# Attention's landmark chain moved to earlier half steps in a fused attention and expert kernel

## The chip, the cores and the metric

The kernel runs on one core of one Trainium2 chip. The metric is the device time of one execution, in microseconds (us); less is better. The core has five engines that run side by side, each through its own queue in order: TensorE (matmuls, PE in the profile; its weight loads are PEld), VectorE (DVE), ScalarE (ACT), GpSimd (POOL) and SyncE (SP), which issues DMAs here.

## The reference

Nyström attention (B = 8, H = 8, S = 576, D = 64, 32 landmarks), then two feed-forward layers:

```
q_lm = q.reshape(B, H, m, S // m, D).mean(axis=3)
k_lm = k.reshape(B, H, m, S // m, D).mean(axis=3)
A = sm(q, k_lm)
Bm = sm(q_lm, k_lm)
C = sm(q_lm, k)
Z = Bm.transpose(0, 1, 3, 2) / (np.linalg.norm(Bm, ord=1, ...) * np.linalg.norm(Bm, ord=np.inf, ...) + 1e-06)
for _ in range(6):
    Z = 2 * Z - Z @ Bm @ Z
x = A @ Z @ C @ v
...
h = (x @ w1) * (x @ w2) @ w3 @ w_out
...
g = elu(h @ w_in2)
out = g @ w_out2
```

All data are float32; sm is the scaled softmax over the last axis.

## The kernel before

The program has three stages. The **start** (to about 120 us) loads and converts the first weights, forms w3 times w_out, and runs the attention of batch 0 in between. The **fused stage** (to about 675 us) goes through 8 batches of 16 units each: a unit multiplies one piece of attention by its own weights (`ab`, lines 695 to 697, 12 matmuls of 288 columns), multiplies the two results (`ab_product`: copy `a` on ScalarE, line 704, product `g` on VectorE, line 706), splits the product of the unit before in two parts (`ab_split`: `gh` on ScalarE, `gl` on VectorE, lines 70 and 71), and multiplies the parts of two units before by w3 (`yy`, lines 722 to 724, 12 matmuls). The **last stage** is the second layer, in 512-token blocks.

While the units of batch b run, the attention of batch b+1 is worked out in pieces, called half steps, two to a unit: the even one stands between `ab` and `yy`, the odd one after `yy`. The table in `steps` says which piece stands at which half step; there is no scheduler behind it, each engine's queue follows from the order in which the program is written. The pieces that matter here:

- `sums` and `q_pad`: landmark sums of queries and keys (VectorE, line 302), their padded copy (ScalarE, line 308).
- The landmark chain: `b_scores` (TensorE, line 353, then maximum and difference on VectorE, lines 359 and 361), `b_exp` (ScalarE, line 365), `b_soft` (four operations on VectorE, lines 371 to 374), `b_norms` (five, lines 378 to 385), `b_norms2` (five, lines 391 to 399), `r0` (TensorE, line 406; X on VectorE, line 408), six times `newton` (`n` on TensorE, line 418; X on VectorE, line 420).
- The keys' part: `c_scores` in two halves (TensorE, line 317; copies `e` on ScalarE, line 328), `c_max` in two (VectorE, lines 334 and 335), `c_exp` in two (ScalarE, line 338), `c_trans` in three (`ct`: TensorE, lines 429 and 432; copy on ScalarE), `c_norm` (VectorE, lines 345 and 347), then `cv` and `zcv`, which join both parts.
- From step 22 on, the queries' scores `a_scores` (line 317 for `a`, transposes at line 488).

`r0` and those Newton steps that fall on an even half step are taken ahead of the rest by `quick`, between `ab` and `ab_product`. Beside the attention, `fill` moves a pipe of weight conversions on by one tick in each half step. A conversion (`join_bits`) starts at half steps 1, 5, 11, 14 and 18 and has its four VectorE operations (lines 169 to 172) three ticks later, at 8 for the one that starts at 5; its GpSimd operations follow one tick after. In the start, the steps of batch 0 run at 1.6 per tick beside `bits_job` (lines 120 to 133). The scores, r0, Newton steps and transposes share two PSUM buffers (pool `ps_at`), taken in turn; `ab` has two others, which the copy `a` and the product `g` free.

Of the kernel before, what the change touches and what calls it, by code (L numbers as in the profile page):

```python
# [64 lines left out]
def nystrom_moe_kernel(ctx, tc, qT, kT, vm, vr, w12, w3T, w_out1, w_in2, w_out2, out):  # L65
# [216 lines left out]
    class Attention:  # L282
# [239 lines left out]
        def steps(self, first=False):  # L522

            s = {}

            def at(i, f, *a):
                s.setdefault(i, []).append((f, a))

            for hp in range(NP):
                at((-16, -14, -12, -11)[hp], self.sums, "k", hp)  # L530
                at(hp, self.sums, "q", hp)
            at(4, self.q_pad)
            at(6, self.b_scores)
            at(7, self.b_exp)
            at(7, self.c_scores, 0)
            at(8, self.c_scores, 1)
            at(8, self.b_soft)
            at(9, self.c_max, 0)
            at(9, self.c_exp, 0)
            at(10, self.b_norms)  # L540
            at(10, self.c_max, 1)
            at(10, self.c_exp, 1)
            at(11, self.b_norms2)
            at(12, self.r0)
            at(13, self.c_norm)
            for k in range(6):
                at(13 + k, self.newton, k)
            for k in range(3):
                at(11 + 2 * k, self.c_trans, k)
            at(18, self.cv, 0)  # L550
            at(19, self.cv, 1)
            at(21, self.zcv)
            when = ((22, 22, 23, 24, 25, 26, 27), (26, 27, 28, 29, 30, 32, 34))
            if first:
                when = ((11, 11, 12, 13, 14, 15, 16), (17, 17, N1, N1 + 1, N1 + 2, N1 + 3, N1 + 4))
            for n, o in enumerate(when):
                at(o[0], self.a_scores, n)
                at(o[1], self.a_max)
                at(o[2], self.a_sub)
                at(o[3], self.a_exp)  # L560
                at(o[4], self.a_sum)
                at(o[5], self.a_mul, n)
                at(o[6], self.a_split, n)
            return s
# [6 lines left out]
    with tc.manual_schedule():  # L571
# [55 lines left out]
        for o in ORDER:  # L627
            if o == "A":
                k, n_wo = n_wo, n_wo + 1
# [389 lines left out]
```

## Time and profile before

| | us |
|---|---|
| median of 3 runs | 1438.42 |
| lowest, highest | 1437.57, 1439.11 |
| the profiled execution | 1436.56 |
| its span, first to last instruction | 1434.4 |

| engine | busy, us | share of the span |
|---|---|---|
| TensorE (PE) | 1370.2 | 96% |
| weight loads (PEld) | 1179.0 | 82% |
| VectorE (DVE) | 1088.0 | 76% |
| ScalarE (ACT) | 630.8 | 44% |
| GpSimd (POOL) | 368.3 | 26% |

Matmuls overlap in the profile, and their ends are modelled: a busy TensorE there is not TensorE at its peak, and the gaps between matmuls say more than the share. A row of a timeline has the start, the length, the engine, the line, the operation, what it writes and reads, and in brackets the idle time of the engine ahead of it with what ended it.

### The profile page before, as it was taken

To read this page: it belongs to the slowest core of one execution; us is meant where nothing else is said; L and a number is where in the kernel's file an instruction comes from. 1 tells how busy PE (TensorE), PEld (TensorE's weight loads), DVE (VectorE), ACT (ScalarE), POOL (GpSimd) and SP (SyncE) were. 2 spreads that over 40 slices of the span, in tenths; PEclk is the share of its full clock that TensorE was granted. 3 is DMA by queue.
4 is the path that set the end of the run, shared out by engine and by line. 5 is a ranking of instruction groups with operands and counts; after the bars stand their busy time and mean duration, and the time that the engine had idled before them with its cause. 6 is when DMAs were issued, how large, how long until landed. Compare 5 with 4: busy or idle time off the path is not lost.

```text
span 1434.4 us, 27127 instructions
## 1 busy us (share of the span) xinstructions
PE 1370.2 (96%) x10848; PEld 1179.0 (82%) x10848; DVE 1088.0 (76%) x2003; ACT 630.8 (44%) x1266; POOL 368.3 (26%) x378
## 2 busy tenths in 40 slices
PE   5786999999999999999999999999999999999998
PEld 2234888888878888899898989999899998999987
DVE  7898687778687787744887878878687887877774
ACT  5444454435344444433444434444344444434442
POOL 4452346344365353420301101010110101011000
PEclk9988999999999999999999999999999999999999
DMA  8643344453635533252966465565645556555440
GB/s 308 234 137 122 121 156 168 165 165 108 207 101 189 204 127 112 102 200 74 414 250 225 165 226 193 188 229 185 210 179 211 207 185 219 198 196 195 177 161 30
DMA packets 56014, 259.70 MB, mean 181 GB/s; under 512 B 5200, under 2 KB 14416, under 8 KB 43600
## 3 DMA queue, kind: packets, MB, share of 16 engines
q0 software_dynamic: 12672, 140.51, 27.2%
q1 hardware_dynamic: 43216, 117.46, 23.5%
q8 instruction: 85, 1.39, 0.4%
q14 instruction: 41, 0.34, 0.1%
HBM read 216.01 MB, written 41.94 MB: 180 GB/s over the span
## 4 chain that ended last, share of the span: by engine, by line
PE 83%; DVE 13%; ACT 1%; issue 1%; DMA 1%; SPq 0%; DVEq 0%; ACTq 0%
PE o L857 9%; PE o L856 9%; PE o L855 9%; PE hm L800 8%; PE hm L801 8%; PE hm L802 8%; PE y L722 5%; PE ab L695 4%; PE ab L696 4%; PE ab L697 4%; PE y L724 4%; PE y L723 4%; PE m L317 2%; DVE w_b L128 1%; DVE w_b L124 1%
## 5 line engine op out<-in xcount | busy, mean ns | idle before, releaser
L800 PE MATMUL hm<-yb,wh 128*128 128x256 f32 x1008 | 285.3, 283 | 3.6 <-ACT s L812 3.5
L801 PE MATMUL hm<-yb,wh 128*128 128x256 f32 x1008 | 285.1, 283 | 0.0
L802 PE MATMUL hm<-yb,wh 128*128 128x256 f32 x1008 | 284.9, 283 | 0.0
L857 PE MATMUL o<-wo,el 128*128 128x512 f32 x576 | 225.6, 392 | 0.0
L856 PE MATMUL o<-wo,eh 128*128 128x512 f32 x576 | 225.3, 391 | 0.0
L855 PE MATMUL o<-wo,eh 128*128 128x512 f32 x576 | 224.0, 389 | 0.0
L831 ACT ACTIVATE t<-m 128x512 f32<-128x512 f32 x144 | 89.9, 624 | 301.4 <-DVE m L829 301.4
L800 PEld LDWEIGHTS hm<-yb,wh 128*128 128x128 f32 x1008 | 192.9, 191 | 6.9 <-ACT s L812 4.0
L746 POOL DMA_DIRECT2D wh<-wh_d x72 | 39.5, 549 | 613.6 <-PE hm L802 607.5
L801 PEld LDWEIGHTS hm<-yb,wh 128*128 128x128 f32 x1008 | 192.9, 191 | 2.8
L802 PEld LDWEIGHTS hm<-yb,wh 128*128 128x128 f32 x1008 | 193.0, 192 | 0.0
L722 PE MATMUL y<-gh,w3oh 128*128 128x288 f32 x512 | 160.5, 313 | 2.9 <-DVE w3ol L71 2.9
L834 DVE SCALAR_TENSOR_TENSOR t<-m,t 128x512 f32<-128x512 f32 x144 | 99.2, 689 | 77.9 <-ACT m L832 77.9
L695 PE MATMUL ab<-ath,mh 128*128 128x288 f32 x512 | 157.2, 307 | 0.9 <-ACT a L704 0.9
L696 PE MATMUL ab<-atl,mh 128*128 128x288 f32 x512 | 151.8, 296 | 0.0
L697 PE MATMUL ab<-ath,ml 128*128 128x288 f32 x512 | 151.1, 295 | 0.0
L724 PE MATMUL y<-gh,w3ol 128*128 128x288 f32 x512 | 151.0, 295 | 0.0
L723 PE MATMUL y<-gl,w3oh 128*128 128x288 f32 x512 | 150.8, 295 | 0.0
L722 PEld LDWEIGHTS y<-gh,w3oh 128*128 128x128 f32 x512 | 96.1, 188 | 39.9 <-issue 22.3
L857 PEld LDWEIGHTS o<-wo,el 128*128 128x128 f32 x576 | 108.1, 188 | 22.7
L855 PEld LDWEIGHTS o<-wo,eh 128*128 128x128 f32 x576 | 108.5, 188 | 20.9
L856 PEld LDWEIGHTS o<-wo,eh 128*128 128x128 f32 x576 | 108.1, 188 | 21.2
(146 smaller groups left out, 2732.4 us busy)
## 6 DMA issues: line engine op xcount, KB each, us to landing
wh<-wh_d POOLq DMA_DIRECT2D x72, 1792.0 KB, 7.8
wo_raw<-in_w_out_dram SPq DMA_DIRECT2D x24, 512.0 KB, 5.4
k<-in_kT_dram SPq DMA_DIRECT2D x8, 1152.0 KB, 6.4
q<-in_qT_dram SPq DMA_DIRECT2D x8, 1152.0 KB, 5.3
yd<-ysb SPq DMA_DIRECT2D x16, 576.0 KB, 3.6
yin<-yd SPq DMA_DIRECT2D x9, 1024.0 KB, 9.9
out_dram<-osb SPq DMA_DIRECT2D x36, 256.0 KB, 2.3
w_raw<-in_w3T_dram SPq DMA_DIRECT2D x16, 512.0 KB, 5.1
```

Source lines behind the costliest of these rows:

```text
L695: pe.matmul(p[:, :NH], mh[:, cs], ah[:, blk, :], start=(blk == 0), stop=False)
L696: pe.matmul(p[:, :NH], mh[:, cs], al[:, blk, :], start=False, stop=False)
L697: pe.matmul(p[:, :NH], ml[:, cs], ah[:, blk, :], start=False, stop=(blk == 1))
L722: pe.matmul(a[oc][:, :NH], w3o_hi[fc][:, os_], gh, start=(fc == 0), stop=False)
L723: pe.matmul(a[oc][:, :NH], w3o_hi[fc][:, os_], gl, start=False, stop=False)
L724: pe.matmul(a[oc][:, :NH], w3o_lo[fc][:, os_], gh, start=False, stop=(fc == K1 - 1))
L800: pe.matmul(o, ah, bh[:, kk, :], start=(kk == 0), stop=False)
L801: pe.matmul(o, ah, bl[:, kk, :], start=False, stop=False)
L802: pe.matmul(o, al, bh[:, kk, :], start=False, stop=(kk == 1))
L855: pe.matmul(a, eh[:, ts_], w[:, 0, :], start=first, stop=False)
L856: pe.matmul(a, eh[:, ts_], w[:, 1, :], start=False, stop=False)
L857: pe.matmul(a, el[:, ts_], w[:, 0, :], start=False, stop=last)
```

## The change

Only numbers in the table of half steps change. The landmark chain moves forward: `b_scores` from 6 to 5, `b_exp` from 7 to 6, `b_soft` from 8 to 7, `b_norms` from 10 to 8, `b_norms2` from 11 to 9, `r0` from 12 to 10, the Newton steps from 13 to 18 to 11 to 16. The transposes `c_trans` move back from 11, 13, 15 to 12, 14, 16 and `c_norm` from 13 to 17. `c_scores`, `c_max` and `c_exp` keep their numbers, but at step 9 `b_norms2` is now written ahead of `c_max`.

```
-            at(6, self.b_scores)
-            at(7, self.b_exp)
+            at(5, self.b_scores)
+            at(6, self.b_exp)
+            at(7, self.b_soft)
             at(7, self.c_scores, 0)
+            at(8, self.b_norms)
             at(8, self.c_scores, 1)
-            at(8, self.b_soft)
+            at(9, self.b_norms2)
             at(9, self.c_max, 0)
             at(9, self.c_exp, 0)
-            at(10, self.b_norms)
+            at(10, self.r0)
             at(10, self.c_max, 1)
             at(10, self.c_exp, 1)
-            at(11, self.b_norms2)
-            at(12, self.r0)
-            at(13, self.c_norm)
             for k in range(6):
-                at(13 + k, self.newton, k)
+                at(11 + k, self.newton, k)
             for k in range(3):
-                at(11 + 2 * k, self.c_trans, k)
+                at(12 + 2 * k, self.c_trans, k)
+            at(17, self.c_norm)
```

VectorE in a steady batch (the attention of batch 3), from the end of the weight conversion at half step 8 (`w_s`, line 172) on; `cb` is the keys' maximum, `bt`, `bst`, `bsb`, `bsx` the first part of the norms. Before:

```order
L172 TENSOR_SCALAR w_s<-w_p 128x512
L334 TENSOR_REDUCE cb_3285<-e_3_3210 128x1
L335 TENSOR_SCALAR cb_3285<-cb_3285 128x1
L706 TENSOR_TENSOR g_3308<-ab_1_3299,a_3306 128x288
L71 TENSOR_TENSOR gl_3245<-g_3242,gh_3244 128x288
L378 STREAM_TRANSPOSE bt_3314<-bm_3195 128x64
L380 TENSOR_REDUCE bst_3316<-bm_3195 128x2
L381 TENSOR_REDUCE bst_3316<-bt_3314 128x2
L383 COPY bsb_3319<-bst_3316 128x128
L385 STREAM_TRANSPOSE bsx_3321<-bsb_3319 128x128
L334 TENSOR_REDUCE cb_3285<-e_3_3211 128x1
```

The same place in the change; `bmm` and `brc` are the second part of the norms, and the second X is the one from r0:

```order
L172 TENSOR_SCALAR w_s<-w_p 128x512
L391 TENSOR_REDUCE bmm_3294<-bsx_3260 128x4
L394 TENSOR_TENSOR brc_3296<-bmm_3294 128x2
L395 TENSOR_SCALAR brc_3296<-brc_3296 128x2
L396 RECIPROCAL brc_3296<-brc_3296 128x2
L399 TENSOR_TENSOR X_3300<-bm_3168,brc_3296 128x2x32
L334 TENSOR_REDUCE cb_3302<-e_3_3215 128x1
L335 TENSOR_SCALAR cb_3302<-cb_3302 128x1
L408 TENSOR_TENSOR X_3300<-r_3_3323,brc_3296 128x2x32
L706 TENSOR_TENSOR g_3335<-ab_1_3316,a_3333 128x288
L71 TENSOR_TENSOR gl_3250<-g_3247,gh_3249 128x288
L334 TENSOR_REDUCE cb_3302<-e_3_3216 128x1
```

The first part of the norms now stands ahead of the conversion, and the second part, the first maximum and X stand between the conversion and the next unit's product.

ScalarE at the same place in the change, from the copies of the keys' second scores on; `w_t` belongs to the conversion, and line 338 is the exponential that waits for `cb`:

```order
L328 COPY e_3_3215<-c_3_3262 128x288
L328 COPY e_3_3216<-c_3_3263 128x288
L167 ACTIVATE w_t<-w_raw 128x512
L338 ACTIVATE e_3_3215,csum_3303<-e_3_3215,cb_3302 128x576
L704 COPY a_3333<-ab_0_3309 128x288
L70 CAST gh_3249<-g_3247 128x288
L338 ACTIVATE e_3_3216,csum_3303<-e_3_3216,cb_3302 128x576
L704 COPY a_3398<-ab_0_3373 128x288
```

This order is as before up to the second exponential; a copy of `ct` that stood behind it is now further back.

TensorE in the start, where the second half of the queries' scores `a` begins. Before:

```order
L585 MATMUL w3acc_442<-wo_311,w_672 128x512
L585 MATMUL w3acc_443<-wo_311,w_672 128x512
L418 MATMUL n_0_733<-X_693 32x64 x8
L317 MATMUL a_0_745<-q_155,ksum_247 32x288
L317 MATMUL a_0_746<-q_155,ksum_247 32x288
```

And in the change:

```order
L432 MATMUL ct_0_718<-ident,e_0_381 64x128
L585 MATMUL w3acc_449<-wo_311,w_687 128x512
L585 MATMUL w3acc_450<-wo_311,w_687 128x512
L585 MATMUL w3acc_451<-wo_311,w_687 128x512
L585 MATMUL w3acc_452<-wo_311,w_687 128x512
L317 MATMUL a_0_756<-q_155,ksum_247 32x288
```

A Newton step stood right ahead of the scores; now all six are over by then.

## Rows read from the trace of the kernel before

**Rows 1.** TensorE's waits, 170 to 600 us: total, times, longest (us).
```profile
PE n L418 <- DVE X L408: 4.5, 4, 1.7
...
PE ct L429 <- ACT e L338: 2.8, 3, 1.3
```

**Rows 2.** Timeline of TensorE in the batch at 256 to 325 us.
```profile
285.07 0.60 PE L429 MATMUL ct<-ident,e 128*128 128x128 f32 x4
...
287.17 0.33 PE L406 MATMUL r<-bt 32*32 32x32 f32 x16
...
290.93 0.43 PE L418 MATMUL n<-X 32*32 32x64 f32 x16 [1.65 <-DVE X L408]
```

**Rows 3.** Timeline of VectorE in the same batch.
```profile
280.47 0.21 DVE L371 TENSOR_REDUCE bsum<-bm 128x2 f32<-128x64 f32 x1
...
281.26 0.29 DVE L169 TENSOR_SCALAR w_y<-w_y 128x512 uint16<-128x512 uint16 x1
...
282.71 0.29 DVE L172 TENSOR_SCALAR w_s<-w_p 128x512 uint16<-128x512 uint16 x1
282.92 0.74 DVE L334 TENSOR_REDUCE cb<-e 128x1 f32<-128x576 f32 x1
...
285.87 0.24 DVE L378 STREAM_TRANSPOSE bt<-bm 128x64 f32<-128x64 f32 x1
...
286.91 0.71 DVE L334 TENSOR_REDUCE cb<-e 128x1 f32<-128x576 f32 x1
```

**Rows 4.** Timeline of VectorE in the start, behind a conversion.
```profile
72.55 0.28 DVE L391 TENSOR_REDUCE bmm<-bsx 128x4 f32<-128x128 f32 x1
72.86 0.93 DVE L394 TENSOR_TENSOR brc<-bmm 128x2 f32<-128x2 f32 x1
73.83 1.20 DVE L395 TENSOR_SCALAR brc<-brc 128x2 f32<-128x2 f32 x1
...
75.40 0.84 DVE L488 STREAM_TRANSPOSE at<-a 128x288 f32<-128x288 f32 x2
```

**Rows 5.** Timeline of GpSimd at the same time.
```profile
72.17 1.60 POOL L133 TENSOR_TENSOR w_sb<-w_b,w_r 128x512 uint32<-128x512 uint32 x1 [5.19 <-DVE w_b L128]
```

**Rows 6.** Timeline of VectorE in the batch at 468 to 537 us.
```profile
501.84 0.28 DVE L391 TENSOR_REDUCE bmm<-bsx 128x4 f32<-128x128 f32 x1
...
502.89 0.22 DVE L408 TENSOR_TENSOR X<-r,brc 128x64 f32<-128x64 f32 x1
```

**Rows 7.** Timelines of ScalarE (a copy) and TensorE (a waiting ab).
```profile
284.72 0.38 ACT L704 COPY a<-ab 128x288 f32<-128x288 f32 x1
...
403.26 0.40 PE L695 MATMUL ab<-ath,mh 128*128 128x288 f32 x1 [0.93 <-ACT a L704]
```

**Rows 8.** Timelines of VectorE and TensorE, first and last of six batches.
```profile
215.60 0.29 DVE L172 TENSOR_SCALAR w_s<-w_p 128x512 uint16<-128x512 uint16 x1
...
217.76 0.66 PE L429 MATMUL ct<-ident,e 128*128 128x128 f32 x4
...
564.88 0.29 DVE L172 TENSOR_SCALAR w_s<-w_p 128x512 uint16<-128x512 uint16 x1
...
567.27 0.60 PE L429 MATMUL ct<-ident,e 128*128 128x128 f32 x4
```

**Rows 9.** TensorE's waits in the start, 40 to 118 us.
```profile
PE a L317 <- ACT ct L434: 4.2, 1, 4.2
PE a L317 <- DVE X L420: 3.6, 1, 3.6
```

**Rows 10.** Timeline of VectorE in the start, transposes of the second scores.
```profile
99.91 0.85 DVE L488 STREAM_TRANSPOSE at<-a 128x288 f32<-128x288 f32 x2 [1.34 <-PE a L317]
```

**Rows 11.** Windows: stretch, busy time (count) of PE, PEld, DVE, ACT, POOL; clock, DMA.
```profile
94.00:106.00 12.00, 7.74 (x95) 3.67 (x95) 10.62 (x21) 4.29 (x7) 5.27 (x5) 0.72 0.42 144
130.00:136.00 6.00, 4.98 (x31) 3.51 (x31) 5.86 (x11) 4.08 (x9) 2.60 (x2) 0.72 0.61 176
170.00:600.00 430.00, 417.79 (x4593) 357.76 (x4594) 333.22 (x734) 195.13 (x465) 205.15 (x199) 1.00 0.45 155
```

## The prediction

> **What bounds the kernel now.** I read the list of busy shares first, then TensorE's waits in the stretch of the steady batches, then one batch in the timelines of TensorE, VectorE, ScalarE and GpSimd, and last the start. TensorE sets the time of the fused stage: its matmuls there follow each other at a fixed pitch, and only where another engine is late does a gap open. So the worth of the change in batches 2 to 7 is the sum of such gaps before and after. The waits of TensorE between 170 and 600 us [rows 1] hold two that belong to the landmark chain: the first Newton step n waits for X, line 408, 4.5 us in four batches, and the first key transpose ct waits for the exponential e, line 338, 2.8 us in three. Together 7.3 us, which is all that the change can take away there. The third large wait, m for "at" (line 488), belongs to steps 22 and later, which stay.
>
> [Rows 2] show one batch: ct at half step 11, r0 between, then n, 1.65 us late for X. VectorE is late there because within two half steps it has to pass norms, a maximum, the second part of the norms, and then X.
>
> **What moves, and what VectorE then has in its queue.** The steps keep their instructions; no DMA is added or taken away, and the queues of SP and POOL hold the same rows. What changes is the place relative to a step that does not move: the weight conversion, whose four VectorE operations stand at the end of half step 8 (lines 169 to 172). Before, the softmax stood ahead of the conversion, and the maximum of the keys' first half (line 334) right behind it. Now the first part of the norms stands ahead, and behind the conversion come the second part of the norms, then the maximum, then X from r0. That is so in all six batches 2 to 7. So X, which n at half step 11 wants, and the maximum, for which the exponential waits, are both behind more work than before. I work out when the next unit's ab can start, from the start of L172, the conversion's last operation:
>
> - Softmax out, norms in ahead of the conversion: 281.26 - 280.47 = 0.79 us out, 286.91 - 285.87 = 1.04 us in: 0.25 us later [rows 3].
> - From L172 to the operation behind it: 282.92 - 282.71 = 0.21 us [rows 3].
> - Second part of the norms: the trace has it right behind a conversion once, in the start: from 72.55 to 75.40, 2.85 us [rows 4]. It is long because GpSimd takes up its own addition of the same conversion at 72.17, and the small operation at line 394 (0.93 us for 128x2) ends as that one ends, 72.17 + 1.60 = 73.77 [rows 4, 5]; the next one, line 395, takes 1.20 us. In a quiet place the same piece, from line 391 to X, is 502.89 - 501.84 = 1.05 us [rows 6]. Lower end 1.05, upper 2.85 and another wait; in the new order the piece follows the conversion directly, as in the start, so I take 2.85.
> - From the maximum to the end of the exponential, where ScalarE goes on to the copy a of the unit: 284.72 - 282.92 = 1.80 us [rows 3, 7]. That copy stands behind the exponential in ScalarE's queue in both kernels, and the next ab needs the PSUM bank that a reads.
> - The copy itself 0.38 us; at 403.26 the trace has an ab that waited for just such a copy [rows 7].
>
> Sum 0.25 + 0.21 + 2.85 + 1.80 + 0.38 = 5.49 us after the old start of L172. n itself can go earlier, when X is done, so the copy a is the later of the two and sets the gap.
>
> TensorE would be ready for that ab at the old start of ct (less the wait it had) plus r0 and n, which now stand ahead, 0.33 + 0.43 = 0.76 us [rows 2]. So the batch of [rows 2, 3] comes out at 282.71 + 5.49 - 285.07 - 0.76 = 2.37 us late; the first of the six at 215.60 + 4.73 - 217.76 = 2.57, the last at 564.88 + 4.73 - 567.27 = 2.34 [rows 8]. Worked out so, the six sum to 17.7 us (2.3 to 3.9 each). Against the 7.3 us that go: +10.4 us.
>
> Nothing hides this: the matmuls behind a waiting n stood too, as the gap of 1.65 us shows [rows 2]. What is late next is the second Newton step. Behind the late copy VectorE has the product g, its remainder gl, the second maximum, and only then n's update; this ends about as ab ends. If GpSimd holds gl as it held line 394 (up to 0.93 us), the second step waits that much; four of the batches have more GpSimd work queued then, and I take half of it for each, +2 us, between 0 and 4. From half step 12 on the Newton steps keep their spacing against the conversions as before, and the transposes have three and four half steps after their exponentials where they had two and three: nothing there. The reciprocal of the sums, moved from 13 to 17, lies beside a queue that has room, and its user comes at 19: nothing. The scores at 5 need the queries' padded sums of step 4, and the running maximum of 32 columns fits into VectorE's pause ahead of the next g: nothing.
>
> One rule of the Trainium skill bears on the 2.85 us. It says (page "SBUF — State Buffer", section "SBUF: two separate sides") that VectorE and GpSimd share a port pair as an exclusive lock, held for a whole instruction, taken by whichever starts first, and asked for by a VectorE operation with two SBUF inputs or in a two-port mode. Line 394 ending with GpSimd's addition agrees. By that rule line 399, with two inputs, would be caught a third time wherever GpSimd has a third operation queued, as in four of the six batches; at 0.93 us each that is +3.7 us on the sum, which I leave to the range.
>
> **The start.** Steps run 1.6 to a conversion there. The one wait that goes cleanly is at half step 17: the scores a of the second half hold on for the update of a Newton step, 3.6 us [rows 9], because that step holds a PSUM buffer and its update stands behind a conversion. Now Newton is over by 16. But VectorE reaches the transposes of a only after the same conversion: they waited 1.34 us for TensorE [rows 10], less 0.21 us for a small operation that now stands ahead (a step of this size is in [rows 3]): -1.1 us, counted as if all of it reaches the end of the start. The wait of a for ct, 4.2 us [rows 9], goes too, but the longer norms behind the earlier conversion and a transpose queue of equal length take its place; I set it at nothing, and bound the start by -7.8 (both waits) and +2 us. Batch 1, whose conversions are others, I set at nothing, within 1 us either way.
>
> **Sum.** 10.4 + 2 - 1.1 = 11.3 us. On the profiled execution, 1436.56 us, that is 1447.9; the median of the runs shown, 1438.42, stands 1.86 us above it, so 1449.7 us.
>
> **Rivals.**
> *The port is free.* If GpSimd's additions start later than VectorE's small operations, the second part of the norms takes 1.05 us. Each batch is then 1.80 us less late, 17.7 - 10.8 = 6.9, 0.4 less than what goes away; with the start 1438.42 - 0.4 - 1.1 = 1436.9 us. Against it: the two orders in which the engines arrive are 0.1 us apart and VectorE came second in the start. It decides at line 394.
> *The start pays.* If the start ends as soon as TensorE has its scores, both waits there, 4.2 + 3.6 = 7.8 us, come off. With the price of the forecast this is still 10.4 + 2 - 7.8 = +4.6, 1443.0 us; with a free port too it is 1438.42 - 0.4 - 7.8 = 1430.2 us, faster. It needs VectorE to have room in the start, and it is nearly always busy there, so this is unlikely.
> *The clock falls.* After the 3.6 us wait of a [rows 9], the stretch from 94 to 106 us shows a granted clock of 0.72 on average, between the levels of 2.4 and 1.2 GHz, which is 12 x 0.28 = 3.4 us lost; 130 to 136 shows 0.72, 1.7 us lost [rows 11]. The new gaps of 2.3 to 3.9 us are of that size, with only n's small matmuls in them. Three falls at 1.7 to 3.4 would give 1454.8 to 1459.9, six short ones 1459.9. Against it: from 170 to 600 us, with the waits of [rows 1] in it, the clock stands at 1.00 [rows 11]. The Trainium skill speaks for it (page "TensorE: Matmul & The Clock Gate", section "HAM oscillation — how this bites in real kernels"): bursts parted by waits bring the engine back slow each time; no steady batch here shows it yet.
>
> **How the numbers follow.** Forecast 0.58, clock 0.22, free port 0.12, the start with a free port 0.08. About 0.2% (2.9 us) is what a measurement of this kernel can tell from no change. Slower by more: forecast and clock and a little of the free port, 0.82; within: 0.10; faster: 0.08. The range goes from 1440, a port that is free in most batches, to 1461, six falls of the clock.
>
> **What would show it.** TensorE's wait of n for X should be there in all six batches, 2 us or so, followed by a wait of ab for a of 0.5 to 1; the wait of ct for e gone; lines 394, 395 at 0.5 to 1.2 us each right behind line 172; start of the fused stage about 1 us earlier. Wrong if n's wait vanishes, if lines 394 and 395 take below 0.2 us, or if the start moves by more than 3 us.

## The result and the profile after

The changed kernel takes 1454.39 us (median of 4 runs, 1452.42 to 1455.96); the kernel before, in the same comparison, 1437.99 us (1437.44 to 1439.11). The ratio is 1.0116, with a 95% interval of 1.0101 to 1.0132: slower by 16 us, where 1449.7 us was forecast, in a range of 1440 to 1461. The profiled execution took 1455.96 us with a span of 1454.2 us, 19.8 us more than the span before; it is the slowest of the four.

TensorE's waits in the changed kernel, 170 to 615 us, are the first thing to set beside [rows 1] (who waits for whom, then total, times and longest, in us):

```profile
PE n L418 <- DVE X L408: 11.3, 6, 2.6
PE ab L695 <- ACT a L704: 4.2, 7, 0.9
```

The wait of ct for e is gone, as the change meant it. The wait of n for X went from 4.5 us in four batches to 11.3 in all six, and a second one came behind it: ab for the copy a, 0.9 us before (the one row with it in [rows 7]), 4.2 now. So TensorE stands 7.6 us longer in those six batches: 6.8 for n, 3.3 for ab, 0.3 for the second Newton step (n for X at line 420), less the 2.8 of ct.

VectorE in the batch of [rows 2, 3], now some 4 us later, from the conversion's last operation on (start, length, operation):

```profile
286.88 0.29 DVE L172 TENSOR_SCALAR w_s<-w_p 128x512 uint16<-128x512 uint16 x1
287.09 0.28 DVE L391 TENSOR_REDUCE bmm<-bsx 128x4 f32<-128x128 f32 x1
287.40 1.09 DVE L394 TENSOR_TENSOR brc<-bmm 128x2 f32<-128x2 f32 x1
288.53 0.17 DVE L395 TENSOR_SCALAR brc<-brc 128x2 f32<-128x2 f32 x1
288.74 0.17 DVE L396 RECIPROCAL brc<-brc 128x2 f32<-128x2 f32 x1
288.94 0.87 DVE L399 TENSOR_TENSOR X<-bm,brc 128x64 f32<-128x64 f32 x1
289.73 0.74 DVE L334 TENSOR_REDUCE cb<-e 128x1 f32<-128x576 f32 x1
...
290.58 0.21 DVE L408 TENSOR_TENSOR X<-r,brc 128x64 f32<-128x64 f32 x1
```

GpSimd at the same time:

```profile
287.32 1.16 POOL L174 TENSOR_TENSOR w_t<-w_t,w_s 128x512 f32<-128x512 f32 x1 [5.79 <-DVE w_s L172]
288.56 1.16 POOL L176 TENSOR_TENSOR wx<-w_t,w_p 128x512 f32<-128x512 f32 x1
```

The operation at line 394, two numbers per partition, starts 0.08 us after GpSimd's first operation and ends as that one ends (287.32 + 1.16 = 288.48). Line 395 then starts at 288.53, 0.03 us ahead of GpSimd's second operation, and takes its own 0.17 us; line 399 falls into that second one and ends 0.09 us behind it. So the second part of the norms, from 287.09 to 289.73, takes 2.64 us, and X comes after the maximum. The other five batches show the same lengths to 0.02 us.

ScalarE and TensorE there:

```profile
290.75 0.78 ACT L338 ACTIVATE e<-e,cb 128x576 f32<-128x576 f32 x1 [5.14 <-DVE cb L335]
...
291.53 0.38 ACT L704 COPY a<-ab 128x288 f32<-128x288 f32 x1
```

```profile
290.94 0.43 PE L418 MATMUL n<-X 32*32 32x64 f32 x16 [1.28 <-DVE X L408]
291.96 0.40 PE L695 MATMUL ab<-ath,mh 128*128 128x288 f32 x1 [0.59 <-ACT a L704]
```

n is 1.28 us late for X, and the ab behind it another 0.59, because ScalarE waited 5.14 us for the maximum, with the copy a behind it in its queue.

The waits are 7.6 of the 19.8 us. The rest shows in the windows (stretch, busy times with counts, then clock, DMA share, GB/s): five falls of the granted clock between 170 and 620 us, each in its stretch of 10 us, against none between 170 and 600 us before [rows 11].

```profile
220.00:230.00 10.00, 9.40 (x100) 8.43 (x98) 4.08 (x13) 4.64 (x13) 0.00 (x0) 0.83 0.19 75
360.00:370.00 10.00, 8.01 (x77) 7.09 (x78) 4.32 (x13) 4.11 (x10) 4.37 (x5) 0.66 0.78 249
440.00:450.00 10.00, 9.47 (x99) 8.65 (x100) 4.61 (x12) 4.25 (x13) 1.38 (x3) 0.83 1.01 354
510.00:520.00 10.00, 6.81 (x76) 5.84 (x78) 5.58 (x15) 4.12 (x10) 1.71 (x2) 0.83 0.36 142
580.00:590.00 10.00, 8.16 (x89) 7.12 (x88) 7.39 (x18) 3.39 (x9) 7.20 (x8) 0.84 0.20 54
```

Each lies right behind one of the late n. Apart from the waits of n and ab, TensorE is busy there, but at 1.2 GHz for a part: 10 x (0.17 + 0.34 + 0.17 + 0.17 + 0.16) = 10.1 us lost. Only the batch at 290 us kept its clock. A sixth fall came in the last stage, where a wait that the kernel before has too (2.77 us, hm for s) took the clock down in this execution and not in that one:

```profile
692.00:710.00 18.00, 14.95 (x93) 14.40 (x94) 14.86 (x26) 8.09 (x15) 6.39 (x12) 0.81 0.98 355
```

At the first matmul of that stage that waits (hm for s, 0.76 us in both) the changed kernel is 692.28 - 674.78 = 17.5 us behind; the stage itself takes 2.3 us more (1454.2 - 692.28 against 1434.4 - 674.78). 7.6 + 10.1 + 2.3 = 20.0, against 19.8 us. The 2.3 are not laid to the change: the clock falls at that wait in ten of the thirteen profiles here, with either table, and not in three, the kernel before among them. The start and batch 1 together come out at 0.25 us less (the first y, line 722, of the 17th unit, just ahead of batch 2's chain, starts at 204.36 before and 204.11 now), and that hides two parts. TensorE at the start of the fused stage, before and after:

```profile
127.96 0.40 PE L722 MATMUL y<-gh,w3oh 128*128 128x288 f32 x1 [0.65 <-DVE w3ol L71]
...
150.72 0.66 PE L429 MATMUL ct<-ident,e 128*128 128x128 f32 x4 [2.18 <-DVE ml L479]
```

```profile
125.17 0.40 PE L722 MATMUL y<-gh,w3oh 128*128 128x288 f32 x1 [0.65 <-DVE w3ol L71]
...
131.21 1.10 PE L317 MATMUL m<-w_sb,z 64*32 64x512 f32 x7 [0.88 <-DVE bm L361]
```

The start gains 127.96 - 125.17 = 2.8 us, and by 204 us 2.5 of it are lost again: in batch 1 the scores now stand ahead of the m tiles of half step 5, and m waits for bm. Windows from the first y to the third unit's, before and after:

```profile
126.40:142.30 15.90, 11.71 (x114) 8.50 (x113) 13.63 (x26) 9.72 (x22) 6.44 (x5) 0.89 0.34 100
```

```profile
123.60:141.30 17.70, 13.94 (x114) 8.95 (x112) 14.42 (x26) 9.65 (x22) 6.24 (x5) 0.81 0.31 90
```

The same 114 matmuls take 1.8 us longer, and the clock can account for most of it: 17.7 x 0.19 - 15.9 x 0.11 = 1.6 us, less what fell into m's wait.

### The profile page after: what moved, and what is told of

It reads as the page before. It is cut to its first block, busy times and chain, and to the rows that moved or that the text cites. A ratio compares the mean times of both kernels' runs of the same rounds, so it can differ in the third digit from the quotient of the medians.

```text
span 1454.2 us, 27139 instructions
## 1 busy us (share of the span) xinstructions
PE 1382.4 (95%) x10848; PEld 1189.1 (82%) x10848; DVE 1104.0 (76%) x2003; ACT 631.3 (43%) x1266; POOL 367.6 (25%) x378
## 4 chain that ended last, share of the span: by engine, by line
PE 61%; DVE 1%; ACT 0%; issue 0%; DVEq 0%; ACTq 0%
PE o L857 9%; PE o L856 9%; PE o L855 9%; PE hm L800 8%; PE hm L801 8%; PE hm L802 8%; PE y L722 1%; PE ab L695 1%; PE y L724 1%; PE y L723 1%; PE ab L696 1%; PE ab L697 1%; PE m L317 1%; DVE gl L71 0%; PE a L317 0%; PE n L418 0%
```

## The experiments

The theory behind the first four: gaps come from small VectorE operations that GpSimd holds, and from the maximum and its exponential in front of X and of a; the gaps take the clock down. The rivals: the slow stretches are something else, the conversion as such is in the way, the chain's place as such is at fault.

**Filling the gap.** Only the clock can gain from this; the added results are never read.

```
             o = 0 if it < 5 else ML
+            if it == 0 and self.b >= 2:
+                for _ in range(10):
+                    pe.matmul(p[:, 128:416], w3o_hi[0][:, 0:128], w3o_hi[1][:, 0:288], start=True, stop=True)
```

> The changed kernel with ten extra matmuls of 288 columns (operands that are long in place, result never read) right ahead of the first Newton step of batches 2 to 7, some 1.33 us of TensorE work per batch inside the gap. Theory (gaps, and a clock that falls because of them): the granted clock stays at 1.00 from 200 to 600 us, the falls of about 10 us go, n still starts when X is there; 1443 to 1447 us. Rival (the slow stretches have another cause): the same clock falls stay, 1453 to 1457. Second rival (TensorE is not really waiting there): +8 us, 1462.

Measured: 1447.73 us, ratio 1.0069 (1.0054 to 1.0084), against the changed kernel's 1.0116: 6.8 us less, with 60 matmuls more. TensorE's waits and the clock from 170 to 600 us (lines from 415 on stand 3 further down in this kernel):

```profile
PE n L421 <- DVE X L408: 2.2, 4, 1.0
PE n L421 <- DVE X L423: 1.2, 3, 0.5
```

```profile
170.00:350.00 180.00, 177.92 (x1896) 152.29 (x1895) 148.81 (x309) 82.44 (x196) 80.69 (x78) 1.00 0.46 157
350.00:450.00 100.00, 93.56 (x1011) 80.01 (x1010) 72.40 (x153) 40.77 (x99) 44.55 (x46) 0.97 0.48 160
450.00:600.00 150.00, 147.02 (x1641) 126.45 (x1642) 122.28 (x259) 68.45 (x164) 73.88 (x70) 1.00 0.39 134
```

The waits of n shrink by about what the added matmuls fill, six times 1.33 us, so TensorE waits or fills for as long as before; what went is the clock's part, all but 3 us between 350 and 450 (two falls, behind the n at 360 us and behind m's wait for at of 2.17 us at 401). The second rival, that TensorE has no gap there, would have cost 8 us, and falls. The time is 0.7 us above the forecast of 1443 to 1447.

**The norms ahead of the conversion.** The queue ahead of X keeps its number of operations.

```
             at(8, self.b_norms)
+            at(8, self.b_norms2)
...
-            at(9, self.b_norms2)
```

> The changed kernel with the second part of the norms at half step 8, ahead of the weight conversion instead of right behind it; the number of VectorE operations ahead of X is the same. Theory (the small operations are long because GpSimd's additions hold them): lines 394, 395, 399 fall from about 1.1, 0.2, 0.9 to 0.2 us each, the gaps of n and ab together from 14.6 to about 5 us, clock falls rarer; 1436 to 1442 us. Rival (it is the count of operations in VectorE's queue, not the holding): gaps stay, 1451 to 1456.

Measured: 1437.33 us, ratio 0.9997 (0.9988 to 1.0007): the whole loss is gone, with one step moved by one. The edit acts in batches 0 and 1 too: the first y of the 17th unit starts at 201.89 us instead of 204.11, so 2.2 us come from there and some 15 from the six batches. The same five operations, in the batch at 421 us, and the conversion behind them:

```profile
423.14 0.29 DVE L391 TENSOR_REDUCE bmm<-bsx 128x4 f32<-128x128 f32 x1
423.46 0.16 DVE L394 TENSOR_TENSOR brc<-bmm 128x2 f32<-128x2 f32 x1
...
424.06 0.23 DVE L399 TENSOR_TENSOR X<-bm,brc 128x64 f32<-128x64 f32 x1
424.20 0.29 DVE L169 TENSOR_SCALAR wo_y<-wo_y 128x512 uint16<-128x512 uint16 x1
```

```profile
PE ab L695 <- ACT a L704: 3.5, 6, 0.6
...
PE n L418 <- DVE X L408: 2.6, 3, 1.3
```

From 423.14 to 424.20 they take 1.06 us, as in a quiet place before [rows 6]. n waits 2.6 us instead of 11.3; ab for a stays at 3.5, since the exponential still stands ahead of a. So the length of the held operations, not the number of operations in VectorE's queue, made most of n's wait.

**The conversion out of the way**, in the changed kernel and in the one before:

```
-CONV = (1, 5, 11, 14, 18)
+CONV = (1, 4, 11, 14, 18)
```

> The changed kernel with the second weight conversion of a batch started at half step 4 instead of 5, so that its VectorE operations stand at the end of 7, where VectorE pauses for about 3 us, and not between the two parts of the norms. Theory (the harm is the conversion in the chain's way): gaps of n and ab below 3 us in total, clock at 1.00, 1430 to 1436 us. Rival (the chain is late by its own length and by the maximum ahead of X): gaps still above 8 us, 1445 or more.

> The kernel before with the same move of the conversion. Theory (the conversion's place decides, not the chain's): the waits of ct for e (2.8 us) and most of n for X (4.5 us) go here too, 1431 to 1435 us, within 2 us of the changed kernel with the same move. Rival (the chain's earlier half steps have a worth of their own once the conversion is away): no change of more than 2 us here, and the changed kernel with the move is faster than this one by 3 us or more.

Measured: 1450.85 us, ratio 1.0089 (1.0074 to 1.0104), for the changed kernel, and 1436.42 us, 0.9994 (0.9982 to 1.0006), for the one before. Both theories missed. For the changed kernel the rival's number came true (1445 us or more), but a chain late by its own length is what the run before spoke against, and the rows show another reason: with the conversion a half step earlier its GpSimd operations are earlier too, and now lie on both parts of the norms. VectorE and GpSimd in the moved version of the changed kernel:

```profile
285.44 0.67 DVE L383 COPY bsb<-bst 128x128 f32<-128x128 f32 x1
...
286.80 0.74 DVE L394 TENSOR_TENSOR brc<-bmm 128x2 f32<-128x2 f32 x1
287.58 0.67 DVE L395 TENSOR_SCALAR brc<-brc 128x2 f32<-128x2 f32 x1
...
288.49 0.64 DVE L399 TENSOR_TENSOR X<-bm,brc 128x64 f32<-128x64 f32 x1
```

```profile
284.76 1.26 POOL L176 TENSOR_TENSOR wx<-w_t,w_p 128x512 f32<-128x512 f32 x1
...
286.79 0.74 POOL L224 TENSOR_TENSOR wx<-wx 128x256 f32<-128x256 f32 x1
287.49 0.74 POOL L226 TENSOR_TENSOR wx<-wx 128x256 f32<-128x256 f32 x1
288.30 0.74 POOL L227 TENSOR_TENSOR wx<-wx 128x256 f32<-128x256 f32 x1
```

Four operations end with a GpSimd operation each. In this batch n still waits 0.89 us, in all six 7.8, and the second Newton step waits 1.15 us here and in the last of the six. So moving the conversion out of the chain's way helps little while its GpSimd work still meets the chain. In the kernel before the move only traded waits, as that run's rival had it (no change of more than 2 us): ct for e 2.5 us, n for X 1.9, and 1.8 of the scores c for their copies, which it did not have.

**The keys' maxima behind the chain**, alone (first) and together with the norms at 8 (second):

```
-            at(9, self.c_max, 0)
-            at(9, self.c_exp, 0)
...
+            for k in range(2):
+                at(11 + k, self.c_max, k)
+                at(11 + k, self.c_exp, k)
             for k in range(3):
-                at(12 + 2 * k, self.c_trans, k)
+                at(13 + 2 * k, self.c_trans, k)
```

> The changed kernel with only the keys' maxima, exponentials and transposes moved back by two, two and one half steps; the second part of the norms stays right behind the conversion. It parts the two causes. Theory (both count, the holding by GpSimd for the larger part of n): n waits 5 to 7 us instead of 11.3, ab for a nearly nothing instead of 3.3, fewer falls of the clock; 1440 to 1446 us. Rival (the maximum and the exponential were the whole cause): no gaps, 1431 to 1436. Rival (the holding was the whole cause): as the changed kernel, 1451 to 1456.

> The changed kernel with the second part of the norms at half step 8 (as in the run before) and the keys' maxima and exponentials at 11 and 12 instead of 9 and 10, their transposes at 13, 15 and 17. Theory (what is left of the gaps, 2.6 us of n and 3.5 us of ab, is the first maximum ahead of X on VectorE and its exponential ahead of the copy a on ScalarE): both waits below 1 us in total, no fall of the clock between 200 and 600 us, 1429 to 1433 us. Rival (the maxima make a new wait where they now stand, at the second and third Newton step or at the transposes): new waits of 4 us or more, 1436 to 1440.

Measured: alone 1435.68 us, ratio 0.9994 (0.9985 to 1.0004); both 1429.10 us, ratio 0.9943 (0.9926 to 0.9959), faster than either kernel. TensorE's waits, alone and both (lines from the table on stand one higher):

```profile
PE n L418 <- DVE X L408: 6.4, 6, 1.9
```

```profile
PE ab L694 <- DVE g L705: 1.2, 1, 1.2
PE ab L694 <- ACT a L703: 0.9, 1, 0.9
PE n L418 <- DVE X L408: 0.9, 1, 0.9
```

Alone, the wait of ab for a is gone and n waits 6.4 us, as expected; the time is 4 us below the forecast. Two things stand behind that. The clock fell only near 391 and 497 us; and 4.3 us were won ahead of the six batches, in the start and batch 1, where the edit acts too (the first y of the 17th unit at 199.83 us instead of 204.11), which the forecast had left out. With both, 0.9 us of n's wait is left and the clock stands at 1.00 from 170 to 600 us:

```profile
170.00:600.00 430.00, 422.75 (x4630) 360.94 (x4615) 350.66 (x739) 195.48 (x467) 203.19 (x195) 1.00 0.44 151
```

By the ratios, moving the norms takes 17 us off the changed kernel, moving the maxima 18, both together 25: each alone leaves two falls of the clock where there were five, so the parts do not add up. By the same y, 2.2, 4.3 and 5.7 us of this come ahead of the six batches (it starts at 198.40 us with both).

**Which batches.** The new table for batch 0 alone, and for batches 2 to 7 alone (diff of the first; in the second the condition is `not first and self.b > 1`):

```
+            if first:
+                at(5, self.b_scores)
...
+            else:
+                at(6, self.b_scores)
```

> The new table for batch 0 alone, the old one for batches 1 to 7. Theory (the start gains 2 to 3 us and batch 1 gives them back, because its VectorE and GpSimd work on conversions sets its pace): fused stage starts near 118 us instead of 120.8, the first step of batch 2 within 1 us of before; 1437 to 1439 us. Rival (the giving back comes from the new table in batch 1, the scores ahead of the m tiles): the gain of the start stays, 1434.5 to 1436.

> The new table for batches 2 to 7 alone, the old one for batches 0 and 1. Theory (the harm is made in those six batches: 7 us of waits more and falls of the clock, some 17 us): the fused stage reaches batch 2 as before and then loses as the changed kernel does; 1451 to 1456 us. Rival (a good part of the harm comes from the start or batch 1): below 1448.

Measured: batch 0 alone 1434.56 us, ratio 0.9986 (0.9977 to 0.9996); batches 2 to 7 alone 1454.83 us, ratio 1.0110 (1.0094 to 1.0126). The second says that the six batches make the whole loss. The first was expected the other way: the start's gain stays, when batch 1 has the old table. TensorE there:

```profile
147.63 0.66 PE L429 MATMUL ct<-ident,e 128*128 128x128 f32 x4 [2.17 <-DVE ml L479]
```

ct comes at 147.63 instead of 150.72, so the 3 us of the start are kept; in the changed kernel batch 1 itself gives them back. The start's gain is known to about 1 us: in the second run, with the start as before, the y that came at 127.96 comes at 127.06.

**Batch 1's scores** back behind the m tiles, in the changed kernel and in the fastest version:

```
-            at(5, self.b_scores)
+            at(6 if self.b == 1 else 5, self.b_scores)
```

> The changed kernel with the landmark scores of batch 1 alone back at half step 6, so that they stand behind the m tiles of half step 5 and not ahead of them. Theory (in batch 1 the m tiles wait for VectorE's maximum of the scores, which share their two PSUM buffers, and this eats the gain of the start): the wait of m for bm (0.9 us) goes, 1 to 3 us less than the changed kernel, 1451 to 1453. Rival (the gain of the start is eaten by the conversions anyway, or later in batch 1): within 1 us of the changed kernel.

> The fastest version so far (second part of the norms at 8, the keys' maxima at 11 and 12) with the scores of batch 1 back at 6. Theory as in the run before: 1 to 3 us below that version's 1429.1, 1426 to 1428 us. Rival: the same within 1 us.

Measured: 1452.80 us, ratio 1.0099 (1.0084 to 1.0113), and 1427.62 us, ratio 0.9926 (0.9911 to 0.9941). Both intervals overlap those without the edit (1.0116 and 0.9943), so a gain of 1 to 2 us is not shown, and the profiles don't show it either: from the first y to the 17th unit's batch 1 takes 80.0 us against 80.5 in the changed kernel, and 78.7 against 78.0 in the fastest. The wait of m for bm went, and another took its place:

```profile
135.25 0.33 PE L353 MATMUL bs<-ksum,qpad 128*32 128x32 f32 x16 [2.72 <-DVE ml L479]
```

The kernel before has this wait too, at 1.31 us. The scores and the m tiles share two PSUM buffers; whichever comes second waits for VectorE.

**The softmax alone.** The kernel before with three steps earlier:

```
-            at(6, self.b_scores)
-            at(7, self.b_exp)
+            at(5, self.b_scores)
+            at(6, self.b_exp)
+            at(7, self.b_soft)
...
-            at(8, self.b_soft)
```

> The kernel before with only scores, exponential and softmax of the landmarks one half step earlier (5, 6, 7); norms, Newton steps and transposes as before. Theory (the softmax leaves VectorE's queue ahead of the conversion and the first maximum comes about 0.8 us earlier): the waits of ct for e fall from 2.8 to below 1 us, those of n for X stay at 3 to 5; 1435 to 1437 us. Rival (GpSimd's additions come earlier too and hold other operations): no change within 1 us, 1437 to 1439.

Measured: 1433.65 us, ratio 0.9975 (0.9966 to 0.9985).

```profile
PE n L418 <- DVE X L408: 2.4, 3, 0.9
PE ct L429 <- ACT e L338: 1.3, 2, 0.7
```

Both waits fell, ct from 2.8 to 1.3 us and, unlike the forecast, n from 4.5 to 2.4; so the time is 1.4 us below the forecast. This part of the change is good by itself: the softmax goes where VectorE pauses, and nothing comes in its place behind the conversion. The fall of n goes with the held operations: in the batch at 288 us lines 394, 395 and 399 take 0.16, 0.60 and 0.38 us here, against 0.74, 0.53 and 1.17 in the kernel before.

## Why the prediction was right, and where not

The direction, the mechanism and the place were right: in all six batches n waits for X behind held norms and a maximum, and ab for a behind the exponential. By its steps:

- *2.85 us for the second part of the norms:* 2.64 in the batch of [rows 2, 3]. Line 395 was forecast held and slipped through, 0.03 us ahead of GpSimd; so line 399 met GpSimd's second operation, and a third held one did not come in any of the six batches. The rule of the Trainium skill on this (page "SBUF — State Buffer", section "SBUF: two separate sides") agrees with these rows: line 394 took 1.09 us held and 0.16 us free.
- *1.80 us from the maximum to a:* 291.53 - 289.73 = 1.80.
- *a gap of 2.37 us in that batch, 17.7 us in six:* 1.28 + 0.59 = 1.87 there, 11.3 + 3.3 = 14.6 us in six. This term was 3 us too large, 1.3 of it by line 395 (six times 0.21). The gaps that went measured 7.3, as said.
- *+2 us for the second Newton step:* 0.3 us, in one batch. gl was held 0.3 us there, and elsewhere not at the wrong time.
- *The start, -1.1, and batch 1, nothing:* -2.8 and, given back in batch 1, +2.5. The step that failed here is "batch 1 I set at nothing": the scores were put ahead of the m tiles with two PSUM buffers between them, and the m tiles' turn on these was not followed, nor the clock there.
- *The clock:* the step that failed most. It was set aside as a rival at 0.22, on the ground that from 170 to 600 us no wait had taken the clock down [rows 11]. That ground was one execution: m's wait for at of 2.17 us in it was, in other kernels, followed by a fall in eight of the thirteen profiles here. Five falls cost 10.1 us in the profile, and filling the gap took 6.8 us off; the time is close to the low end of that rival, 1454.8. Each late n now has a wait of ab behind it, with only 16 small matmuls between. That this succession is what takes the clock down is not shown: with the maxima moved, a fall came behind a single wait of n of 1.91 us. The rule of the Trainium skill cited there (page "TensorE: Matmul & The Clock Gate", section "HAM oscillation — how this bites in real kernels"), that bursts parted by waits bring the engine back slow, is borne out by the five falls, stretches at 0.66 to 0.84; the batch at 290 us, which kept its clock, shows that it is not so each time.

So the forecast of 1449.7 lies 4.7 us low because two errors partly cancel, and so close a figure is in part luck: the waits grew by 7.6 us where 12.4 were summed, and the clock, not in the sum, took 10.

One reading of the kernel before stopped short. It laid the late X to what VectorE has to pass; but in that batch GpSimd held the small operations already:

```profile
288.04 0.74 DVE L394 TENSOR_TENSOR brc<-bmm 128x2 f32<-128x2 f32 x1
288.81 0.53 DVE L395 TENSOR_SCALAR brc<-brc 128x2 f32<-128x2 f32 x1
...
289.58 1.17 DVE L399 TENSOR_TENSOR X<-bm,brc 128x64 f32<-128x64 f32 x1
```

In a free place they take 0.16, 0.17 and 0.23 us, so 1.88 us are held, and n waited 1.65. The four batches in which n waits for X in the kernel before are the four with such held operations; in the other two all three are short and n does not wait. So the 4.5 us of n that were to go had the same cause as most of the 11.3 that came.

*The port is free* fell at line 394, as it said it would. *The start pays* came true for 2.8 of its 7.8 us, and batch 1 took most of these back.

What stays open: why the clock stays low longer in batch 1 of the changed kernel. It does (6.8 us at 1.2 GHz behind the first y) in all seven profiles in which m waits for bm, but in two of the other six too. The edit that was tried moved the wait and gave 1 to 2 us, inside the intervals.

## What to carry to other kernels

Before putting a chain of tiny VectorE operations somewhere, look at what GpSimd runs at that moment: an operation on two columns cost 1.09 us behind a GpSimd addition and 0.16 us away from it, and the cure was to put the chain ahead of the work that feeds GpSimd; moving that work by half a step was none. Count as late also what stands behind the late one in another engine's queue: the exponential that waited for the maximum kept ScalarE from a copy that frees a PSUM bank. And price a new gap on TensorE at more than its length, even where the profile before shows gaps nearly as long that left the clock alone, for that profile is one execution: here 7.6 us of waits brought 10 us of slow clock.

## What the runs showed of the hardware that was not expected

The clock fell after gaps no longer than ones that had left it alone, and not each time. In the changed kernel the gap at 217 to 220 us (1.56 and 0.60 us) took it down and the one at 290 us (1.28 and 0.59) did not; with the new table in batches 2 to 7 alone, the same gap near 290 did:

```profile
290.00:300.00 10.00, 8.13 (x88) 7.07 (x87) 4.80 (x13) 4.20 (x11) 5.25 (x7) 0.83 0.25 79
```

A single wait of m for at of 2.15 to 2.17 us, which all thirteen profiles have between 386 and 405 us, was followed by a fall in eight of them (0.83 over 10 us) and by none in five, the kernel before and the changed one among these. That such falls make the times of one program differ is not shown: the kernel before, with none from 170 to 600 us in its profile, gave 1435.72 to 1440.85 us over 19 executions.

Which of the small operations are held was not all known: 128x2 with two inputs (line 394) and 128x2 with a constant (395) are, and so is the copy of 128x128 at line 383, 0.67 us against 0.23; the reciprocal on 128x2 (396) and the operation with a constant on 128x1 (335) were not, in any batch of the thirteen profiles.
